# Second block of an output projection by seven products, with other places and queues around it

## The chip, the cores and the metric

The kernel runs on one core of a Trainium2 chip. The metric is the device time of one execution in microseconds (us). The engines are named as in the profile: PE multiplies matrices, DVE, ACT and POOL do elementwise work, SP issues most of the DMAs; ACT and POOL have DMA queues of their own.

## The reference

The kernel computes a gated mix of attention and a layer of 64 experts, for 2048 tokens of width 1024. Cut to what matters:

```python
g = sigmoid((x * gate_w).sum(-1, keepdims=True))
q, k, v = split_heads(x @ wqkv)                    # 32 heads of width 32
a = heads(softmax(q k^T / sqrt(32)) @ v) @ wo      # attention, then its output projection
b = sum over heads of gelu(x . u[e]) * v[e]        # e: the best of 8 x 8 keys of that head
out = g * a + (1 - g) * b
```

## The kernel before, in words

Numbers of 32 bits are split into two parts, hi and lo, by the helper `split` (ACT copies the hi part, L95; DVE subtracts it to get lo, L96). A product of two such numbers is three matmuls: hi by hi, hi by lo, lo by hi.

The program runs through six stages on one core. First the projections of q and k (L291 a first plain piece, L303 the rest), then the router of the experts (L726), the values (L965 and L984), 32 heads of attention (L1319 scores, L1329 exponentials, L1340 weights times values, L1369 row sums), and the output projection (L1522, L1529, L965). The gate and the experts' weighted sum lie among them. PE's order is the order in which the code calls `matmul`; each engine works through its own instructions in that order, and semaphores hold an instruction until what it reads is written and what it overwrites is read. DMAs go by the helper `dma` (L77) on the queue of SP unless another is given, and are issued in the order of the code too; within a queue each issue can wait, and then all behind it wait.

A product of two matrices cut in halves is computed in two ways here. The plain way takes eight products of halves. `Halves` takes seven (P1 to P7): sums of quarters of the left factor (S1 to S4) with sums of quarters of the right factor (T1 to T4), then a chain of additions on DVE (`tt`, L971) that puts the four quarters of the result together:

```python
tt(u2, c1, p6); tt(u3, u2, p7); tt(u2, u2, p5); tt(u5, u3, p5)
```

where `c1` is a copy of P1; `c1` plus P2, `u2` plus P3, `u3` plus P4 and `u5` (in the output stage plus the experts' share) are then stored. P1, P2, P3, P4 use A11, A12, S4, A22; P5, P6, P7 use S1, S2, S3.

**The start.** The first weights are two tiles of 128x128, one that becomes `A` and one that becomes `S` (both `wraw`), on ACT's queue; x comes on SP's. PE multiplies an identity (L409) seven times while they load, as its first work, and then begins L291.

**The values' last unit.** `values_unit(u)` runs for u = 0 to 5. Its results go through four places, `c1`, `u2`, `u3` and `u5` of `work` (in the profile `xh`), and are stored to `vd`. In the last unit (`last`), `first_scores` (L1225) issues the first four matmuls of attention between P2 and P4.

**The output.** The 2048 rows are worked in eight blocks of 256. `wo` is held as `woh` and `wol`, split from `wo_raw`. A block's attention result is loaded as `V` (`OC[n]`, by `load_o`), its reciprocal row sums times the gate as `rb` or `accd` (`RB[n]`, by `load_rb`), and multiplied (L1549, L1576, L1591). The reciprocals of the last group of four heads are the last of all: `norm_r(G - 1)` computes them on DVE (L1402, L1403), a DMA stores them to `rd`, and `load_rb(n, KC - 1, KC)` loads them for the last K step of blocks 0 and 1. Blocks 0 and 1 are computed the plain way (`wo_mm`: eight K steps of 12 matmuls, and eight of `av_mm` for the experts' share, 104 in all); blocks 2 to 7 by `unit(n)` with seven products of 12 and the same eight, 92 in all. The places of the results, `post`, lie in the first block's `rb` and are four pieces of 512: `plain_out` fills all four for blocks 0 and 1, `unit` uses three of them and `osb`. The `T1` to `T4` come from memory (`t0h`, `t0l` to `t3h`, `t3l`, each 1 MB in all or in four pieces).

Of the kernel before, what the change touches and what calls it, by code (L numbers as in the profile page):

```python
# [16 lines left out]
S = 2048  # L17
D = 1024
H = 32
KC = D // 128  # L20
# [11 lines left out]
def gated_mha_peer_kernel(ctx, tc, xT, wqkv, wv, wo, wq, k12, ug, v, out):  # L32
# [42 lines left out]
    def dma(dst, src, queue=nc.sync):  # L75
        a, b = (ap.bitcast(F32) if ap.dtype == F32R else ap for ap in (dst, src))
        return queue.dma_start(a, b)  # L77
# [289 lines left out]
    w0 = wr.tile([128, 2, KC, 128], F32, name="wraw")  # L367
    wraw[0] = raw_quarters(w0)

    def load_w0(k0, k1, queue=nc.sync):  # L370
        for w in range(2):
# [19 lines left out]
    for name in ("B11", "B12", "B21", "B22"):  # L391
        X[name] = x_parts(PASS[0][name], None, xp)

    load_w0(0, 1, nc.scalar)
    load_x(0, 0, 2)
    load_w0(1, 2)
    load_x(0, 1)
# [7 lines left out]
    plain_banks(0)  # L405


    for i in range(7):
        nc.tensor.matmul(b0[1, 1][:, :128], ident, ident, start=True, stop=True)  # L409
    dma(gw, ug.rearrange("p (k m) -> p k m", k=KC)[:, :, 64:65], nc.gpsimd)  # L410
    dma(kraw, k12.rearrange("p (a e) -> p a e", a=2), nc.gpsimd)
# [731 lines left out]
    pso = None  # L1143

    def values_unit(u):
        c1, u2, u3, u5 = (work[k] for k in ("c1", "u2", "u3", "u5"))
        last = u == NU - 1
        order = (("P1", "P2", "P3", "P7", "P5", "P6", "P4") if u == 0 else
                 ("P1", "P7", "P5", "P6", "P3", "P2", "P4") if last else
                 ("P1", "P7", "P5", "P6", "P2", "P3", "P4"))  # L1150
        p, done = {}, set()

        def out(j, half, t, queue=nc.sync):
            dma(VD[half][(2 * u + j) * 128:(2 * u + j + 1) * 128, :], t, queue)

        for k, name in enumerate(order):
            if last and name == "P4":

                nonlocal pso
                ps1.close()  # L1160
                pso = Pool("pso", space=PSUM, side="right")
            p[name] = hv.product(name, bank=pv_bank if last and name == "P4" else None)
            if last and name == "P2":
                first_scores()
            if name == "P1":
                nc.scalar.activation(c1, p[name], AF.Copy)
                hv.rows(x_raw[(u + 1) % 2])
                if u + 2 < NU:
                    load_x_raw(u + 2)
            if name == "P6":  # L1170
                tt(u2, c1, p["P6"])
                tt(u3, u2, p["P7"])
                tt(u2, u2, p["P5"])
                tt(u5, u3, p["P5"])
                out(1, 1, u5)
            if "P6" in p:
                if "P2" in p and "C11" not in p:
                    p["C11"] = tt(c1, c1, p["P2"])
                    out(0, 0, c1)
                if "P3" in p and "C12" not in p:  # L1180
                    p["C12"] = tt(u2, u2, p["P3"])
                    out(0, 1, u2)
            if name == "P4":
                tt(u3, u3, p["P4"])

                out(1, 0, u3, nc.gpsimd if last else nc.sync)

            if u + 1 < NU:
                if k == (4 if u == 0 else 0):
                    hv.parts("A11")  # L1190
                    for s in ("S3", "S1", "S2", "S4"):
                        hv.sums(s)
                    done = {"P1"}
                if k >= 5 or u > 0:
                    for q in ("P7", "P5", "P6", "P2", "P3", "P4"):
# [201 lines left out]
        R[g] = wk.tile([128, 128], F32, name="rr", bufs=1)[:, :64]  # L1397
        dma(R[g], SMD[g].rearrange("j (b m) -> (j b) m", m=64))

    def norm_r(g):  # L1400
        r = R.pop(g)
        nc.vector.reciprocal(r, r)  # L1402
        nc.vector.tensor_mul(r, r, G64)  # L1403
        dma(RD[:, :, g, :].rearrange("j n (q m) -> (j n) q m", m=64), r)


    OC, RB = {}, {}
# [13 lines left out]
    def load_chunk(n, k0, k1, queue=nc.sync):  # L1421
        load_o(n, k0, k1, queue)
        load_rb(n, k0, k1, queue=queue)
# [148 lines left out]
    def scale_o(n):  # L1572

        for k in range(2):
            o = OC[n][:, k * HC:(k + 1) * HC]
            nc.vector.tensor_mul(o, o, RB[n][:, k * HC:(k + 1) * HC])  # L1576
        ht.rows(OC[n])
# [16 lines left out]
    def banks4():  # L1594
        return {(i, half): bank() for i in range(W // 128) for half in range(2)}
# [29 lines left out]
    load_t(2, None, [fin.tile([128, S], F32R, name="t3l")])  # L1625
    OH[1] = zp.tile([128, KC, W], F32R, name="z1")
    OL[1] = wk.tile([128, KC, W], F32R, name="acc")
    split_o(1, 0, HC)
    split_o(0, KC - 1, KC)
    load_o(2, 0, KC)  # L1630
    load_t(0, *([keep.tile([128, S], F32R, name=f"wo_raw{j}")] for j in range(2)))
# [6 lines left out]
    load_t(2, [zp.tile([128, S], F32R, name="z0")], None)  # L1638
    load_t(1, *([keep.tile([128, S], F32R, name=f"wo_raw{2 + j}")] for j in range(2)))
    load_rb(3, 0, KC)  # L1640
    load_o(3, 0, KC)
# [5 lines left out]
    load_t(3, *([part[k][:, 512:] for k in range(HC)] for part in (woh, wol)))  # L1647
    ht.places(wk.tile([128, S], F32R, name="acc"), "A11", "A12")
    ht.places(fin.tile([128, S], F32R, name="s31"), "S3", "S1")
    scale_o(2)  # L1650
    for name in ("A11", "S3", "S1", "A12"):
        ht.operand(name)
    wo_mm(pa1, 1, [KC - 1], False, True)
    ht.places(zp.tile([128, S], F32R, name="z1"), "S2")
    ht.places(wk.tile([128, S], F32R, name="acc"), "S4", "A22")
    load_at(3)
    ht.b.update({f"B{i + 1}{j + 1}": [[part[i * HC + k][:, j * 512:(j + 1) * 512] for k in range(HC)]
                                    for part in (woh, wol)] for i in range(2) for j in range(2)})

    def osb():  # L1660
        return wk.tile([128, 512], F32, name="osb")

    def unit(n):


        u2, u3, u5 = (post[:, i] for i in range(3))
# [7 lines left out]
                    scale_o(n + 1)  # L1674
                ht.operand(name)

        p1 = ht.product("P1")
        c1 = osb()
        nc.scalar.activation(c1, p1, AF.Copy)
        if n == 2:  # L1680
            ht.operand("S2")
            plain_out(1, pa1)
            for name in ("S4", "A22"):
                ht.operand(name)
        if n + 2 < S // W:
            load_chunk(n + 2, 0, KC)
            load_at(n + 2)
        ahead("A11")
        p7 = ht.product("P7")
        ahead("S3")  # L1690
        p5 = ht.product("P5")
        ahead("S1")
# [3 lines left out]
        tt(u2, u2, p5)  # L1696
        tt(u5, u3, p5)
        ahead("S2")

        def c11():  # L1700
            p2 = ht.product("P2", lambda ps: av_mm(n, 0, 0, ps, first=True))
            pieces = 2 if last else 1
            for i in range(pieces):
                c = slice(i * 512 // pieces, (i + 1) * 512 // pieces)
                tt(c1[:, c], c1[:, c], p2[:, c])
                store(n, 0, 0, c1, c)

        def c12():
            p3 = ht.product("P3", lambda ps: av_mm(n, 0, 1, ps, first=True))
# [12 lines left out]
            store(n, 1, 0, u3)  # L1722

        if not last:
            c11()
            ahead("A12")
        c12()
        ahead("S4")
# [43 lines left out]
```

## Time and profile before

| | |
|---|---|
| median of three runs (lowest, highest) | 1823.78 us (1823.51, 1824.25) |
| profiled execution: time | 1824.35 us |
| profiled execution: span | 1822.6 us |
| PE busy in the span | 1813.3 us, 99% |
| DVE, ACT, POOL busy | 1461.6, 1313.3, 228.7 us |

A row of the timeline gives start, duration, engine, line, operation, the names of output and inputs (buffer numbers left out) with their shapes, how many instructions it joins, and in brackets the idle time before it with what ended it. The rows of waits give the engine and line that waited, what for, total us, times, and the longest. Rows of windows give, for a stretch of time, its length, each engine's busy time with its instructions, the granted clock of PE, the share of DMA and the GB/s. SPq, ACTq and POOLq are the parts of an engine that issue DMAs.

### The profile page before, as it was taken

How to read it: one execution, taken by the hardware profiler on the slowest of the kernel's cores; microseconds unless marked ns; L12 is line 12 of the kernel's file. 1: busy time of each engine (PE TensorE's matmuls, PEld its weight loads, DVE VectorE, ACT ScalarE, POOL GpSimd, SP SyncE). 2: the span in 40 equal slices, each digit the busy share in tenths (PEclk: the TensorE clock that was granted, in tenths of full speed). 3: DMA queues.
4: the chain of work that ended last, by engine and by line, in shares of the span. 5: the costliest groups of instructions: out<-in, count | busy, mean ns of one | idle time of the engine just before them, and what ended most of it. 6: DMA issues, size and time to landing. Idle time of an engine off the chain costs nothing.

```text
span 1822.6 us, 26388 instructions
## 1 busy us (share of the span) xinstructions
PE 1813.3 (99%) x10075; PEld 1098.9 (60%) x10075; DVE 1461.6 (80%) x1258; ACT 1313.3 (72%) x1716; POOL 228.7 (13%) x351
## 2 busy tenths in 40 slices
PE   9999999999999999999999999999999999999999
PEld 6777777788888644444444444444444444447887
DVE  7865966789967788888888888888888888897674
ACT  6544644522333699999999999999999999994221
POOL 1222212244101100000000000000000000000000
PEclk9999999999999999999999999999999999999999
DMA  7888689660267778777788877878787778866641
GB/s 267 281 277 277 214 288 295 197 220 13 81 231 245 224 162 181 151 174 167 166 176 173 181 164 175 170 171 189 159 184 171 161 166 181 186 149 239 256 156 58
DMA packets 117072, 345.23 MB, mean 189 GB/s; under 512 B 16112, under 2 KB 49552, under 8 KB 96016
## 3 DMA queue, kind: packets, MB, share of 16 engines
q1 hardware_dynamic: 87608, 196.28, 36.3%
q0 software_dynamic: 27888, 145.00, 34.7%
q10 hardware_dynamic: 1448, 2.24, 0.3%
q8 instruction: 80, 1.31, 0.3%
q14 instruction: 48, 0.39, 0.1%
HBM read 171.76 MB, written 72.36 MB: 134 GB/s over the span
## 4 chain that ended last, share of the span: by engine, by line
PE 94%; issue 2%; DVE 2%; DMA 1%; ACT 0%; POOL 0%; ACTq 0%; DVEq 0%; POOLq 0%; SPq 0%
PE ring L1319 29%; PE o L1340 26%; PE bk L303 15%; PE pa L965 6%; PE bk L726 5%; PE bk L291 3%; PE pa L1522 2%; PE bk L984 2%; PE bk L965 2%; PE bk L342 2%; PE ring L1353 1%; PE pa L1529 1%; DVE xh L971 1%; DMA t1l<-xl 1%; PE bk L191 0%
## 5 line engine op out<-in xcount | busy, mean ns | idle before, releaser
L1329 ACT ACTIVATE P<-ring 128x1024 f32<-128x1024 f32 (+2 forms) x1031 | 913.1, 983 | 13.1
L1369 DVE TENSOR_TENSOR acc<-acc,P 128x2048 f32<-128x2048 f32 x319 | 731.0, 2292 | 74.5 <-ACT P L1329 49.0
L1340 PE MATMUL o<-P,V 128*32 128x512 f32 x3840 | 464.8, 599 | 0.0
L1319 PE MATMUL ring<-Q,K 98*128 98x512 f32 x1024 | 271.7, 407 | 0.1
L1319 PE MATMUL ring<-z,z 98*128 98x512 f32 x1020 | 270.4, 407 | 0.6 <-ACT accd L1329 0.6
L1319 PEld LDWEIGHTS ring<-Q,K 98*128 98x128 f32 x1024 | 182.1, 188 | 143.7 <-ACT P L1329 73.5
L1319 PEld LDWEIGHTS ring<-z,z 98*128 98x128 f32 x1020 | 181.5, 188 | 142.3 <-ACT P L1329 72.3
L1340 PEld LDWEIGHTS o<-P,V 128*32 128x32 f32 x3840 | 98.8, 109 | 223.4 <-issue 214.5
L1362 POOL DMA_DIRECT2D accd<-P x95 | 81.5, 858 | 928.4 <-PE ring L1319 303.8
L1367 DVE TENSOR_TENSOR acc<-P,P 128x2048 f32<-128x2048 f32 x32 | 73.4, 2293 | 72.5 <-ACT P L1329 72.5
L303 PE MATMUL bk<-xh,A 128*128 128x512 f32 x336 | 82.8, 396 | 0.0
L303 PE MATMUL bk<-xh,S 128*128 128x512 f32 x336 | 81.3, 393 | 0.0
L303 PE MATMUL bk<-xl,S 128*128 128x512 f32 x336 | 80.1, 391 | 0.0
L136 ACT ACTIVATE hi<-u 128x512 fp32r<-128x512 f32 x42 | 26.5, 632 | 72.8 <-DVE u L513 36.1
L303 PEld LDWEIGHTS bk<-xh,A 128*128 128x128 f32 x336 | 62.0, 188 | 23.8 <-issue 5.0
L1372 DVE TENSOR_TENSOR acc<-acc,accd 128x2048 f32<-128x2048 f32 x32 | 73.1, 2285 | 0.0
L303 PEld LDWEIGHTS bk<-xl,S 128*128 128x128 f32 x336 | 62.8, 188 | 16.3 <-issue 1.7
L303 PEld LDWEIGHTS bk<-xh,S 128*128 128x128 f32 x336 | 62.4, 188 | 14.5 <-issue 1.7
L1329 ACT ACTIVATE accd<-ring 128x1024 f32<-128x1024 f32 (+2 forms) x64 | 62.2, 1032 | 2.3 <-PE ring L1319 2.2
L965 PE MATMUL pa<-woh,acc 128*128 128x512 f32 x192 | 62.2, 389 | 0.0
L513 DVE TENSOR_TENSOR u<-u,bk 128x512 f32<-128x512 f32 x70 | 46.6, 683 | 12.2 <-DMA wpd<-u 7.6
L730 ACT ACTIVATE xu<-bk 128x64 f32<-128x64 f32 x16 | 3.6, 223 | 61.4 <-PE bk L726 61.4
(301 smaller groups left out, 2209.6 us busy)
## 6 DMA issues: line engine op xcount, KB each, us to landing
accd<-P POOLq DMA_DIRECT2D x95, 1024.0 KB, 7.8
wqt<-in_wq SPq DMA_DIRECT2D x64, 512.0 KB
wraw<-in_wqkv SPq DMA_DIRECT2D x28, 512.0 KB
kdh<-hi POOLq DMA_DIRECT2D x32, 256.0 KB, 6.3
kdl<-lo POOLq DMA_DIRECT2D x32, 256.0 KB, 7.0
qdh<-hi POOLq DMA_DIRECT2D x32, 256.0 KB, 6.6
qdl<-lo POOLq DMA_DIRECT2D x32, 256.0 KB, 6.5
z<-kdh SPq DMA_DIRECT2D x32, 256.0 KB
```

What stands on the lines that cost most here:

```text
L291: nc.tensor.matmul(b0[w, n], AW[PLAIN[w, ki]][a][:, k, :], X[f"B{ki + 1}{n + 1}"][b][:, k, :], start=first, stop=last)
L303: nc.tensor.matmul(ps, a[i][:, k, :], b[j][:, k, :], start=(k == 0 and i == j == 0), stop=(k == HC - 1 and i == 1))
L513: nc.vector.tensor_tensor(out=out, in0=a, in1=b, op=OP.add)
L726: nc.tensor.matmul(ps, x_part(a, t // 4, kc)[:, tok], b, start=first, stop=last)
L965: nc.tensor.matmul(ps, self.a[a][i][:, k, :], self.b[b][j][k], start=(not first and k == 0 and i == j == 0), stop=(k == HC - 1 and i == 1))
L1319: on_ring(nc.tensor.matmul(ring[:, i, :], K[:98, kt * 128:(kt + 1) * 128], Q[:98, qc * 512:(qc + 1) * 512], start=True, stop=True), i)
L1329: on_ring(nc.scalar.activation(P[h, kt][:, q0 * 512:(q0 + m) * 512].rearrange("p (a m) -> p a m", a=m), ring[:, i:i + m, :], AF.Exp, scale ...
L1340: nc.tensor.matmul(O[h][32 * qc:32 * qc + 32, :], Vt[g][:, kt, 32 * j:32 * j + 32], p[:, qc * 512:(qc + 1) * 512], start=(kt == 0), stop=( ...
L1362: nc.gpsimd.dma_start(ACCD[h], P[h, kt], accum_op=OP.add)
L1367: nc.vector.tensor_add(ACC[h], P[h, 0], P[h, kt])
L1369: nc.vector.tensor_add(ACC[h], ACC[h], P[h, kt])
L1372: nc.vector.tensor_add(ACC[h], ACC[h], ACCD[h])
```

## The change

It has three parts.

1. At the start, the tile that becomes `S` goes on SP's queue, ahead of x, and the one that becomes `A` stays on ACT's; the identity is multiplied eight times.
2. In the values' last unit the four places lie in a buffer of raw x that is free by then (`xw`), not in `work`.
3. In the output, block 1 goes by `unit(1)`. Its P1 and P7 stand ahead of block 0's last K step. Its sum of P1 and P2 goes to the fourth piece of `post` and is made right after P1 and P2, ahead of the next block's scaling. The last reciprocals are stored and loaded on POOL's queue. The other loads stand on SP's queue in another order: all of block 1 at once, T3, T1, T2, then T4 ahead of block 0's stores.

The core of the diff:

```diff
-    load_w0(0, 1, nc.scalar)
+    load_w0(0, 1, (nc.scalar, nc.sync))
...
-    for i in range(7):
+    for i in range(8):
         nc.tensor.matmul(b0[1, 1][:, :128], ident, ident, start=True, stop=True)
...
     def values_unit(u):
+        last = u == NU - 1
         c1, u2, u3, u5 = (work[k] for k in ("c1", "u2", "u3", "u5"))
+        if last:
+            free = x_raw[(u + 1) % 2].rearrange("p k m -> p (k m)").rearrange("p (a m) -> p a m", m=512)
+            c1, u2, u3, u5 = (free[:, k] for k in range(4))
...
-    def norm_r(g):
+    def norm_r(g, queue=nc.sync):
...
-        dma(RD[:, :, g, :].rearrange("j n (q m) -> (j n) q m", m=64), r)
+        dma(RD[:, :, g, :].rearrange("j n (q m) -> (j n) q m", m=64), r, queue)
...
-            load_o(1, 0, KC - 1)
+            load_o(1, 0, KC)
+            load_o(0, KC - 1, KC)
+            load_t(2, [zp.tile([128, S], F32R, name="z1")], [fin.tile([128, S], F32R, name="t3l")])
...
         if kc == HC:
-            norm_r(G - 1)
+            norm_r(G - 1, nc.gpsimd)
+            load_t(0, *([keep.tile([128, S], F32R, name=f"wo_raw{j}")] for j in range(2)))
     for n in range(2):
-        load_chunk(n, KC - 1, KC)
-    load_rb(2, 0, KC)
+        load_rb(n, KC - 1, KC, nc.gpsimd)
     split_lo(KC - 1)
     split(woh[0], wol[0], raw_wo(0))
...
+    load_t(1, *([keep.tile([128, S], F32R, name=f"wo_raw{2 + j}")] for j in range(2)))
...
+    scale_o(1, 0)
+    for name in ("A11", "S3"):
+        ht.operand(name)
+    load_rb(2, 0, KC)
...
     for (i, half), ps in pa.items():
         av_mm(0, i, half, ps)
+    early = ht.product("P1"), ht.product("P7")
     wo_mm(pa, 0, [KC - 1], False, True)
-    split_o(1, HC, KC)
+    scale_o(1, 1)
+    for name in ("A12", "S1"):
+        ht.operand(name)
     load_at(2)
...
-    pa1 = banks4()
-    wo_mm(pa1, 1, list(range(KC - 1)), True, False)
-    for (i, half), ps in pa1.items():
-        av_mm(1, i, half, ps)
-    plain_out(0, pa)
     load_t(3, *([part[k][:, 512:] for k in range(HC)] for part in (woh, wol)))
+    plain_out(0, pa)
...
-    wo_mm(pa1, 1, [KC - 1], False, True)
...
+        def c11():
+            p2 = ht.product("P2", lambda ps: av_mm(n, 0, 0, ps, first=True))
...
+            r = post[:, 3] if n == 1 else c1
...
+        if n == 1:
+            c11()
         ahead("A11")
-        p7 = ht.product("P7")
+        p7 = p7 or ht.product("P7")
...
-    for n in range(2, S // W):
-        unit(n)
+    for n in range(1, S // W):
+        unit(n, *(early if n == 1 else ()))
```

In the values' last unit DVE's rows stand as follows, before. The `bk` and `o` are PE's products, and the six rows from L971 are the seven additions of the last unit.

```order
L96 TENSOR_TENSOR xl0_4607<-xl0_4607,xu_4609 128x512 x2
L971 TENSOR_TENSOR xh3_4587<-xh3_4587,bk1_5393 128x512
L971 TENSOR_TENSOR xh3_4587<-xh3_4587,bk7_5367 128x512
L971 TENSOR_TENSOR xh3_4587<-xh3_4587,bk0_5380 128x512 x2
L971 TENSOR_TENSOR xh3_4587<-xh3_4587,bk2_5411 128x512
L971 TENSOR_TENSOR xh3_4587<-xh3_4587,bk3_5426 128x512
L971 TENSOR_TENSOR xh3_4587<-xh3_4587,o_5462 128x512
```

And the same place now:

```order
L96 TENSOR_TENSOR xl0_4608<-xl0_4608,xu_4610 128x512 x2
L971 TENSOR_TENSOR xw_4450<-xw_4450,bk1_5394 128x512
L971 TENSOR_TENSOR xw_4450<-xw_4450,bk7_5368 128x512
L971 TENSOR_TENSOR xw_4450<-xw_4450,bk0_5381 128x512 x2
L971 TENSOR_TENSOR xw_4450<-xw_4450,bk2_5412 128x512
L971 TENSOR_TENSOR xw_4450<-xw_4450,bk3_5427 128x512
L971 TENSOR_TENSOR xw_4450<-xw_4450,o_5463 128x512
```

Nothing has moved; the places are others.

In the output stage SP's queue stood as follows from the last reciprocals on (`rr` is read back for them, `rd` is where they are stored, `V` a block's attention result).

```order
L77 DMA V<-od 128x1792
L77 DMA rd<-rr 32x4x64
L77 DMA V<-od 128x256
L77 DMA rb_5491<-rd 128x1x256
L77 DMA V<-od 128x256
L77 DMA accd<-rd 128x1x256
L77 DMA accd<-rd 128x1x2048
L77 DMA t3l<-t2l 128x2048
L77 DMA V<-od 128x2048
L77 DMA wo_raw_12582<-t0h 128x2048
L77 DMA wo_raw_12583<-t0l 128x2048
```

Now it stands so, up to the stores of block 0 (behind `V<-od 128x2048` of block 2 follow an `at`, the eight pieces of T4 and then `out<-rb_5492 128x512 x4`):

```order
L77 DMA V<-od 128x2048
L77 DMA V<-od 128x256
L77 DMA z_12462<-t2h 128x2048
L77 DMA t3l<-t2l 128x2048
L77 DMA wo_raw_12535<-t0h 128x2048
L77 DMA wo_raw_12536<-t0l 128x2048
L77 DMA wo_raw_12576<-t1h 128x2048
L77 DMA wo_raw_12577<-t1l 128x2048
L77 DMA accd<-rd 128x1x2048
L77 DMA V<-od 128x2048
```

The three transfers of the reciprocals left SP's queue; POOL's last rows, behind its DMAs of attention, are now:

```order
L1365 DMA accd<-P_12216 128x2048
L1365 DMA accd<-P_12241 128x2048
L77 DMA rd<-rr 32x4x64
L77 DMA rb_5492<-rd 128x1x256
L77 DMA accd<-rd 128x1x256
```

So SP no longer waits for them, and POOL does.

On PE the rows from the experts' share of block 0 (`at` times `vhl`) on were, before, followed at once by block 0's last K step:

```order
L1529 MATMUL pa0_12411<-vhl_5490,at_12454 128x512 x2
L1529 MATMUL pa1_12412<-vhl_5490,at_12454 128x512 x2
L1529 MATMUL pa2_12413<-vhl_5490,at_12454 128x512 x2
L1529 MATMUL pa3_12414<-vhl_5490,at_12454 128x512 x2
L1522 MATMUL pa0_12411<-woh7_12401,z0_12263 128x512
L1522 MATMUL pa1_12412<-woh7_12401,z0_12263 128x512
```

Now P1 of block 1 comes there, then P7, and only then that K step:

```order
L1532 MATMUL pa0_12412<-vhl_5491,at_12455 128x512 x2
L1532 MATMUL pa1_12413<-vhl_5491,at_12455 128x512 x2
L1532 MATMUL pa2_12414<-vhl_5491,at_12455 128x512 x2
L1532 MATMUL pa3_12415<-vhl_5491,at_12455 128x512 x2
L965 MATMUL pa4_12607<-woh0_12410,acc_12580 128x512
L965 MATMUL pa4_12607<-wol0_12411,acc_12580 128x512
```

24 matmuls have moved ahead of the last K step of block 0.

More of the change, by code (lines that the diff above doesn't have):

```diff
@@ L368, in gated_mha_peer_kernel, with load_w0 @@
     wraw[0] = raw_quarters(w0)
-    def load_w0(k0, k1, queue=nc.sync):
-        for w in range(2):
+    def load_w0(k0, k1, queues=(nc.sync, nc.sync)):
+        for w, queue in enumerate(queues):
             dma(w0[:, w, k0:k1], wqkv[w * 8, :, k0 * 128:k1 * 128].rearrange("p (k m) -> p k m", m=128),
@@ L1570, in load_t, with scale_o @@
             ops[n] = [place[:, k * 512:(k + 1) * 512] for place in part for k in range(m)]
-    def scale_o(n):
-        for k in range(2):
+    def scale_o(n, *ks):
+        for k in ks or range(2):
             o = OC[n][:, k * HC:(k + 1) * HC]
@@ L1615, in gated_mha_peer_kernel @@
         if kc == HC:
-            norm_r(G - 1)
+            norm_r(G - 1, nc.gpsimd)
+            load_t(0, *([keep.tile([128, S], F32R, name=f"wo_raw{j}")] for j in range(2)))
     for n in range(2):
-        load_chunk(n, KC - 1, KC)
-    load_rb(2, 0, KC)
+        load_rb(n, KC - 1, KC, nc.gpsimd)
     split_lo(KC - 1)
     split(woh[0], wol[0], raw_wo(0))
[L1625 to L1628, printed above, removed]
+    load_t(1, *([keep.tile([128, S], F32R, name=f"wo_raw{2 + j}")] for j in range(2)))
+    ht.b.update({f"B{i + 1}{j + 1}": [[part[i * HC + k][:, j * 512:(j + 1) * 512] for k in range(HC)]
+                                    for part in (woh, wol)] for i in range(2) for j in range(2)})
+    ht.places(wk.tile([128, S], F32R, name="acc"), "A11", "A12")
+    ht.places(fin.tile([128, S], F32R, name="s31"), "S3", "S1")
+    scale_o(1, 0)
+    for name in ("A11", "S3"):
+        ht.operand(name)
+    load_rb(2, 0, KC)
     split_o(0, KC - 1, KC)
     load_o(2, 0, KC)
-    load_t(0, *([keep.tile([128, S], F32R, name=f"wo_raw{j}")] for j in range(2)))
     ps_odd = Pool("ps_odd", space=PSUM)
@@ L1634, in gated_mha_peer_kernel, with unit @@
         av_mm(0, i, half, ps)
+    early = ht.product("P1"), ht.product("P7")
     wo_mm(pa, 0, [KC - 1], False, True)
-    split_o(1, HC, KC)
+    scale_o(1, 1)
+    for name in ("A12", "S1"):
+        ht.operand(name)
     load_at(2)
[L1638 to L1641, printed above, removed]
-    pa1 = banks4()
-    wo_mm(pa1, 1, list(range(KC - 1)), True, False)
-    for (i, half), ps in pa1.items():
-        av_mm(1, i, half, ps)
-    plain_out(0, pa)
[L1647 to L1652, printed above, removed]
-    wo_mm(pa1, 1, [KC - 1], False, True)
-    ht.places(zp.tile([128, S], F32R, name="z1"), "S2")
+    load_t(3, *([part[k][:, 512:] for k in range(HC)] for part in (woh, wol)))
+    plain_out(0, pa)
+    ht.places(zp.tile([128, S], F32R, name="z0"), "S2")
     ht.places(wk.tile([128, S], F32R, name="acc"), "S4", "A22")
-    load_at(3)
-    ht.b.update({f"B{i + 1}{j + 1}": [[part[i * HC + k][:, j * 512:(j + 1) * 512] for k in range(HC)]
-                                    for part in (woh, wol)] for i in range(2) for j in range(2)})
     def osb():
         return wk.tile([128, 512], F32, name="osb")
-    def unit(n):
+    def unit(n, p1=None, p7=None):
         u2, u3, u5 = (post[:, i] for i in range(3))
@@ L1675, in ahead @@
                 ht.operand(name)
-        p1 = ht.product("P1")
+        def c11():
+            p2 = ht.product("P2", lambda ps: av_mm(n, 0, 0, ps, first=True))
+            pieces = 2 if last else 1
+            r = post[:, 3] if n == 1 else c1
+            for i in range(pieces):
+                c = slice(i * 512 // pieces, (i + 1) * 512 // pieces)
+                tt(r[:, c], c1[:, c], p2[:, c])
+                store(n, 0, 0, r, c)
+        p1 = p1 or ht.product("P1")
         c1 = osb()
         nc.scalar.activation(c1, p1, AF.Copy)
[L1680 to L1683, printed above, removed]
+        if n == 1:
+            for name in ("S2", "S4", "A22"):
                 ht.operand(name)
@@ L1687, in unit @@
             load_at(n + 2)
+        if n == 1:
+            c11()
         ahead("A11")
-        p7 = ht.product("P7")
+        p7 = p7 or ht.product("P7")
         ahead("S3")
@@ L1698, in unit @@
         ahead("S2")
[L1700 to L1706, printed above, removed]
         def c12():
@@ L1724, in unit @@
         if not last:
-            c11()
+            if n > 1:
+                c11()
             ahead("A12")
```

1 line of the change is left out of this document (removed).

## Prediction

> **What bounds the kernel now.** I read the page first: the busy line and the chain of work that ended last.
>
> ```profile
> PE 1813.3 (99%) x10075; PEld 1098.9 (60%) x10075; DVE 1461.6 (80%) x1258; ACT 1313.3 (72%) x1716; POOL 228.7 (13%) x351
> PE 94%; issue 2%; DVE 2%; DMA 1%; ACT 0%; POOL 0%; ACTq 0%; DVEq 0%; POOLq 0%; SPq 0%
> ```
>
> PE is busy in all but 9.3 of 1822.6 us. The next view is PE's waits, in five stretches; 19 to 200, 640 to 1640 and 1640 to the end have no row. 0 to 20 and 200 to 640 have these:
>
> ```profile
> PE bk L291 <- ACT xh L95: 2.1, 1, 2.1
> ...
> PE bk L1225 <- DVE xh L971: 1.0, 1, 1.0
> PE ring L1319 <- ACT accd L1329: 0.6, 1, 0.6
> ```
>
> So from its first real matmul on PE is the bound everywhere, the output included. A microsecond of PE's work or waiting that goes is a microsecond of the end, and a new wait counts in full. I price each part by what it does to PE.
>
> **The start.** The timeline of the first microseconds:
>
> ```profile
> 0.76 0.87 SPq L77 DMA_DIRECT2D xh<-in_xT  x2
> 0.77 0.90 ACTq L77 DMA_DIRECT2D wraw<-in_wqkv  x2
> 1.40 3.36 PE L409 MATMUL bk<-ident 128*128 128x128 f32 x14 [1.40 <-DVE ident L91]
> 4.89 0.31 ACT L95 ACTIVATE A<-wraw 128x128 fp32r<-128x128 f32 x1 [1.91 <-DMA wraw<-in_wqkv]
> 5.25 0.43 SPq L77 DMA_DIRECT2D xh<-in_xT  x1
> 5.96 0.31 ACT L95 ACTIVATE S<-wraw 128x128 fp32r<-128x128 f32 x1 [0.77 <-DMA wraw<-in_wqkv]
> 6.18 1.14 ACT L95 ACTIVATE xh<-xh 128x512 fp32r<-128x512 f32 x2
> 6.84 0.73 PE L291 MATMUL bk<-xh,A 128*128 128x512 f32 x2 [2.08 <-ACT xh L95]
> ```
>
> PE waits for x's hi part; ACT makes that third, after `A` and `S`, and `S` waits for its tile. First on a queue of its own the tile should land with `A`'s, so that `S` follows at about 5.2. x then goes out one issue later (0.43); its first half had landed by 5.25, where SP goes on after a wait that I put to it, so now by 5.7. From ACT's start on x to PE is 6.84 - 6.18 = 0.66. The first matmul comes between 5.42 + 0.66 = 6.1 and 5.7 + 0.66 = 6.36, or at 6.84 if the tile comes no sooner. I take 6.1, a gain of 0.74.
>
> The idle time matters for something else, in the windows:
>
> ```profile
> 7.00:8.00 1.00, 1.00 (x5) 0.82 (x6) 1.00 (x2) 0.95 (x4) 0.72 (x2) 1.00 1.05 362
> 8.00:9.00 1.00, 1.00 (x5) 0.82 (x4) 1.00 (x4) 1.00 (x3) 0.63 (x3) 0.67 1.04 348
> 9.00:10.00 1.00, 1.00 (x3) 0.73 (x3) 1.00 (x3) 0.68 (x3) 0.00 (x0) 0.50 0.99 295
> 10.00:11.00 1.00, 1.00 (x4) 0.78 (x3) 0.93 (x3) 1.00 (x3) 0.00 (x0) 0.50 1.03 336
> 11.00:12.00 1.00, 1.00 (x5) 0.76 (x4) 1.00 (x3) 1.00 (x3) 0.00 (x0) 0.63 1.02 397
> 612.00:615.00 3.00, 1.99 (x9) 1.28 (x9) 2.96 (x5) 1.61 (x4) 0.00 (x0) 1.00 0.40 162
> ```
>
> The granted clock is half for some 3.4 us (0.33 + 0.50 + 0.50 + 0.37 = 1.70 us of full speed lost) after the idle 2.08 us; after 1.01 us idle near 613 it stayed at 1.00. The eighth identity (3.36 / 7 = 0.48) ends at 5.24, so that 0.86 us of idle is left, less than what cost nothing at 613. So I take the slow stretch to go: 1.70. A faster PE meets x's later pieces: ACT starts on the fourth at 12.80, released by its DMA; I leave 0.25 for such waits. The start gives 0.74 + 1.45 = 2.2, and 0.7 if the clock still falls.
>
> [...]
>
> **The values' last unit.**
>
> ```profile
> 609.57 0.68 DVE L971 TENSOR_TENSOR xh<-xh,bk 128x512 f32<-128x512 f32 x1
> 611.87 3.20 DVE L971 TENSOR_TENSOR xh<-xh,bk 128x512 f32<-128x512 f32 x5 [1.62 <-DMA vd<-xh]
> 612.29 0.63 PE L1225 MATMUL bk<-z,z 98*128 98x512 f32 x2
> 613.93 0.73 PE L1225 MATMUL bk<-z,z 98*128 98x512 f32 x2 [1.01 <-DVE xh L971]
> ```
>
> PE's third score matmul needs a bank that DVE's additions free, and these wait for the stores of the unit before, which still read the same places. In other places DVE goes on at 610.25; the additions take 0.64 each (3.20 / 5), and the one that frees the bank, the fourth in all, ends at about 612.2. The third matmul would follow the second: 612.29 + 2 x 0.227 = 612.74, not 613.93. Gain 1.2 (bounds 0.9 and 1.2); the new place is free, since no unit follows. The next row of PE's waits (0.6 at L1319, for ACT) may take up to 0.3 of it.
>
> **The output.** The cost of a matmul is in the chain of waits; then what block 1 and the reciprocals rest on:
>
> ```profile
> 1711.88 13.60 PE pa L965 x60
> ...
> 1656.18 0.60 SPq L77 DMA_DIRECT2D rd<-rr  x1
> 1659.37 0.54 SPq L77 DMA_DIRECT2D rb<-rd  x1
> 1661.61 1.22 DVE L1591 TENSOR_TENSOR V<-V,accd 128x1024 f32<-128x1024 f32 x1
> 1665.48 1.98 PE L1529 MATMUL pa<-vhl,at 128*128 128x512 f32 x8
> 1667.29 1.07 PE L1522 MATMUL pa<-woh,z 128*128 128x512 f32 x4
> ```
>
> 13.60 / 60 = 0.2267. Block 1 takes 92 instead of 104: 12 x 0.2267 = 2.72.
>
> *Covers.* In before's time P1 would run from 1667.29, P7 from 1670.0, block 0's last K step from 1672.7 to 1675.45. P1's factor is ready at about 1664.2 (1661.61 and 1.22 for the scaling, then two parts of a 128x512 tile, 0.68 each as the addition of that size below). The reciprocals on POOL: they were sent at 1656.18; POOL's queue is empty by then. Its transfers take, from issue to landing,
>
> ```profile
> t0h<-xh POOLq DMA_DIRECT2D x4, 256.0 KB, 2.6
> accd<-P POOLq DMA_DIRECT2D x95, 1024.0 KB, 7.8
> ```
>
> I take 5 for each of the two in turn, about the middle, since they are small but SP's queue is full: landed at about 1667, and 1671.7 would do (K step at 1672.7 less about 1.0 for DVE's and ACT's parts). At 7.8 each it is 1671.8, just in time: cost nothing to 0.1.
>
> *The new wait.* The sum of P1 and P2 of block 1 goes to the fourth piece of `post`, from which block 0's fourth store reads. DVE can't begin it until that store has landed, and behind it on DVE stand block 2's scaling, its operands, and the additions that free PE's bank for block 2's P7. The stores now stand behind T4 in SP's queue. How fast that empties:
>
> ```profile
> SPq L77 <- DMA accd<-rd: 3.4, 1, 3.4
> SPq L77 <- DMA V<-od: 2.4, 1, 2.4
> SPq L77 <- DMA wo_raw<-t1h: 2.1, 1, 2.1
> SPq L77 <- DMA wo_raw<-t1l: 2.0, 1, 2.0
> ...
> 1652.97 0.38 SPq L77 DMA_DIRECT2D V<-od  x1
> ```
>
> Each with the issue of about 0.35 that follows: 1 MB takes 2.4, `V` 2.75, `accd` 3.8. `V` of block 1, issued at 1652.97, lands at about 1658 by the 5 us above; six of 1 MB to 1672.6, `accd` to 1676.4, `V` to 1679.2, `at` 0.35, T4 (2 MB) to 1684.4, the stores to about 1686.8; without gaps in the first part some 1685. DVE could otherwise go on at about 1681.7, after P2.
>
> What follows on DVE in a block:
>
> ```profile
> 1702.05 2.35 DVE L1576 TENSOR_TENSOR V<-V,accd 128x1024 f32<-128x1024 f32 x2
> 1709.08 0.68 DVE L971 TENSOR_TENSOR rb<-osb,pa 128x512 f32<-128x512 f32 x1
> 1709.79 2.01 DVE L971 TENSOR_TENSOR rb<-rb,pa 128x512 f32<-128x512 f32 x3
> ```
>
> From scaling to the second addition's end is 8.4 (1702.05 to 1710.46); with the sum itself (0.68) 9.1. A landing at 1684.5 would free P7's bank at 1693.6, where block 2's P7 is due (1667.29 + 116 x 0.2267: three times 12 to the K step's end, the other 68 of block 1 and 12 of block 2's P1). From 1684.5 on each later microsecond is a stall; 1684.5 to 1687.5 gives 0 to 3, and I take 1.5. The output gives 2.7 - 1.5 = 1.2 (bounds +2.7 and -0.5). T4, which P4 of block 1 needs at about 1687.7, has landed by 1684.4; nothing else of block 1 is later.
>
> **Sum.** 2.2 + 1.2 + 1.2 = 4.6. The profiled execution took 1824.35 (1822.6 and 1.75 outside the span) and so would take 1819.75; it lies 0.57 above the median, so the median becomes 1823.78 - 4.6 = 1819.2.
>
> **The rivals.**
>
> *The clock falls all the same* (chance 0.15). Against it: less idle time than the 1.01 at 613, which cost nothing. For it: that is one case, in another phase. Gain 0.7 + 1.2 + 1.2 = 3.1: 1820.7.
>
> *The stores come so late that the twelve matmuls are eaten* (chance 0.13). SP's queue moves over 9 MB ahead of them; every gap in it adds. With a landing from 1687.2 to 1689.1 the output gives 0 to -1.9, and the time is 1820.4 to 1822.3.
>
> *Slower: the reciprocals on POOL come too late* (chance 0.06). PE stands at block 0's last K step with nothing in front but P1 and P7, and DVE's queue stands too, at the scaling by `rb`. PE waits from a landing at 1671.7 on. To eat 2.2 + 1.2 + 2.7 = 6.1 it must come at 1677.8, and to be slower by more than 0.2% (3.65 us) at 1681.5: 12.7 per transfer, against 2.6 to 7.8 in the rows. At 13.5 each the time is 1829. SP's full queue beside it speaks for it, the rows, taken beside much traffic too, against.
>
> *The change does not do what it says at 613* (chance 0.02), since the additions wait for something else than the places: 1.2 less, 1820.4. The row's releaser, a store to `vd`, speaks against.
>
> **How the numbers follow.** A measurement can tell about 0.2%, so faster means below 1820.1. The forecast has 0.64: 1817.7 without stall, 1820.7 with all of 3; 0.59 of it is faster, and 0.05 comes from the first rival, where the clock falls but no stall comes (1819.2). The rest of that rival, the second and the last lie between 1820.4 and 1822.3, so the same. That makes 0.64 faster, 0.30 the same, 0.06 slower. The range goes from 1817.2 (every term at its better bound, 2.5 + 1.2 + 2.7, would be 1817.4) to 1822.0, which leaves out the slower case and the end of the second rival.
>
> **What would show it.** Right: the first L291 at about 6.1 with a clock of 1.00 through the first 15 us; the second pair of L1225 without a wait; a row of PE waiting at L965 of 0 to 3 us at about 1690, released by DVE; no wait at the last K step of block 0. Wrong: a clock of 0.50 again, a wait at `S`, a PE wait at L1525, or one of more than 3 us in the output.

## The result, and the profile after

The change makes the kernel slower: 1827.08 us in the median of 17 runs (1825.30 to 1829.89), against 1823.88 of before in as many; the ratio is 1.0018, interval 1.0011 to 1.0025. The profiled execution of after took 1826.49 us with a span of 1824.4; that of before had 1824.35 and 1822.6. It is one of the quicker executions of after, so the two traces differ by 2.1 us where the medians differ by 3.2.

The busy line and PE's waits of the changed kernel, those of the first 20 us, then those from 1640 us to the end (line, who is waited for, total us, times, longest):

```profile
PE 1812.6 (99%) x10065; PEld 1097.1 (60%) x10065; DVE 1470.1 (81%) x1273; ACT 1314.8 (72%) x1720; POOL 229.8 (13%) x354
...
PE bk L291 <- ACT xh L95: 1.6, 2, 1.2
...
PE pa L965 <- ACT acc L95: 2.1, 1, 2.1
PE pa L965 <- DVE rb L971: 1.3, 1, 1.3
PE pa L965 <- DVE acc L96: 0.3, 1, 0.3
```

PE has ten records fewer (twelve matmuls less, and two records for the eighth identity), and less busy time. The wait at L1225 is gone. But the output, where PE never waited before, now has three waits. They lie together, at the passage from block 1 to block 2. The timeline of the changed kernel there (start, duration, engine, line, output and inputs, in brackets the idle time before and what ended it):

```profile
1688.71 0.69 DVE L971 TENSOR_TENSOR rb<-osb,pa 128x512 f32<-128x512 f32 x1 [8.48 <-PE pa L965]
1689.32 2.35 DVE L1579 TENSOR_TENSOR V<-V,accd 128x1024 f32<-128x1024 f32 x2
1690.57 0.63 ACT L95 ACTIVATE acc<-V 128x512 fp32r<-128x512 f32 x1 [11.15 <-DVE V L1579]
1691.25 0.50 PE L965 MATMUL pa<-woh,acc 128*128 128x512 f32 x1 [2.12 <-ACT acc L95]
1692.33 1.22 PE L965 MATMUL pa<-woh,acc 128*128 128x512 f32 x2 [0.34 <-DVE acc L96]
1696.96 2.01 DVE L971 TENSOR_TENSOR rb<-rb,pa 128x512 f32<-128x512 f32 x3
1697.80 0.47 PE L965 MATMUL pa<-z,s 128*128 128x512 f32 x1 [1.34 <-DVE rb L971]
```

This reads as follows. The first row is the sum of P1 and P2 of block 1, which writes the fourth piece of `post` (`rb`). DVE stood idle for 8.48 us before it. The row puts that down to PE, whose P2 had ended some twelve us earlier (P5, which comes next, began at 1676.73): it is one of those waits in which the engine named had long been done. What DVE did wait for, the experiments show. Block 2's scaling (L1579) and its A11 (ACT, L95) follow at once, and PE's P1 of block 2 at 1691.25, then, after the chain of additions, its P7 at 1697.80.

How much was lost is read from places that both traces have: the start of the experts' share of block 0 and PE's last matmul. In the changed kernel:

```profile
1663.58 1.98 PE L1532 MATMUL pa<-vhl,at 128*128 128x512 f32 x8
...
1820.07 0.39 PE L965 MATMUL pa<-woh,acc 128*128 128x512 f32 x1
```

and the last matmul before:

```profile
1818.48 0.39 PE L965 MATMUL pa<-woh,acc 128*128 128x512 f32 x1
```

PE began the experts' share of block 0 at 1663.58 instead of 1665.48, so the first two parts had won 1.90 (0.61 by 609 us, 1.20 at L1225). Twelve matmuls fewer are 2.72 more. By these P7 of block 2 was due at 1693.6 - 1.90 = 1691.7, with 1693.6 the prediction's time for it. It came at 1697.80: 6.1 us lost, against 4.6 won. The difference, 1.5, is what the last matmul shows: it starts 1.59 later.

### The profile page after: what moved, and what is told of

It reads as the page before. It is cut to its first block, busy times and chain, and to the rows that moved or that the text cites. A ratio compares the mean times of both kernels' runs of the same rounds, so it can differ in the third digit from the quotient of the medians.

```text
span 1824.4 us, 26392 instructions
## 1 busy us (share of the span) xinstructions
PE 1812.6 (99%) x10065; PEld 1097.1 (60%) x10065; DVE 1470.1 (81%) x1273; ACT 1314.8 (72%) x1720; POOL 229.8 (13%) x354
## 4 chain that ended last, share of the span: by engine, by line
PE 98%; DVE 0%; ACT 0%; DMA 0%; issue 0%; SPq 0%; DVEq 0%; ACTq 0%
PE ring L1322 29%; PE o L1343 26%; PE bk L303 15%; PE pa L965 7%; PE bk L965 6%; PE bk L726 5%; PE bk L984 2%; PE bk L291 2%; PE bk L342 2%; PE ring L1356 1%; PE pa L1525 1%; PE pa L1532 1%; PE bk L191 0%; DMA xh<-in_xT 0%; PE bk L359 0%; ACT P L1332 0%
## 5 line engine op out<-in xcount | busy, mean ns | idle before, releaser
L965 PE MATMUL pa<-woh,acc 128*128 128x512 f32 x224 | 74.2, 396 | 2.5 <-ACT acc L95 2.1
L95 ACT ACTIVATE acc<-V 128x512 fp32r<-128x512 f32 x28 | 17.1, 626 | 47.7 <-DVE V L1579 19.6
```

The lines of the kernel that those rows point to most:

```text
L965: nc.tensor.matmul(ps, self.a[a][i][:, k, :], self.b[b][j][k], start=(not first and k == 0 and i == j == 0), stop=(k == HC - 1 and i == 1))
```

## The experiments

**The place of the sum.** Is it the write into the fourth piece of `post` that holds DVE? The sum was left in the tile of P1's copy. (The later sums of block 1 read that copy, so three quarters of block 1 hold another sum here; the run is read for its time.)

```diff
-            r = post[:, 3] if n == 1 else c1
+            r = c1
```

> The changed kernel, with the sum of P1 and P2 of block 1 left in the tile that holds P1's copy instead of the fourth piece of post. Theory (DVE's queue stands at that sum until block 0's fourth store has landed; block 2's scaling and first operand are behind it): PE's waits at block 2's P1 and P7 and the slow clock at 1690 to 1700 go, 6 us less than the changed kernel, about 1819.4 us, 4.5 below before. Rival (block 2's operands come late because the loads stand in another order, whatever DVE does): at least 2 us of waiting stay at P1, 1825 us or more.

Measured: 1820.47 us, ratio 0.9984 (0.9975 to 0.9993), and no row of PE waiting in the output. The theory holds and the rival falls. The same with a second tile of the `osb` kind, so that all four quarters hold their own sums:

```diff
-            r = post[:, 3] if n == 1 else c1
+            r = osb() if n == 1 else c1
```

> The changed kernel, with the sum of P1 and P2 of block 1 in a second tile of the osb kind instead of the fourth piece of post: the same output as the reference. Theory (only the place held DVE): as with the sum in place, 1820.5 us, no PE wait in the output. Rival (the second tile makes P1's copy of block 2 wait, and PE with it): a PE wait at block 2 and 1822 us or more.

Measured: 1820.10 us, ratio 0.9982 (0.9973 to 0.9991), again no such wait. In its timeline DVE no longer stops at the sum:

```profile
1679.86 0.68 DVE L971 TENSOR_TENSOR osb<-osb,pa 128x512 f32<-128x512 f32 x1
1680.46 2.35 DVE L1579 TENSOR_TENSOR V<-V,accd 128x1024 f32<-128x1024 f32 x2
```

The sum runs 8.85 us earlier than in the changed kernel. Against before, one place makes the difference between 3.2 us lost and 3.65 won.

**Each part alone.** Before with one part of the change at a time (the three parts of the diff above).

> Before with the change at the start alone. Theory (x's second K step, not the weights or the clock, sets PE's pace there): 0.6 us below before, about 1823.3 us, with no clock of 0.5 but an idle PE of about 1.2 us at 9 us. Rival (the prediction's sum): 2.2 us below, 1821.7.

> Before with the last values unit's places alone. Theory (the wait of 1.0 us at L1225 is for the stores from those places): 1.2 us below before, about 1822.7 us, and no row of PE waiting for DVE there. Rival (PE then waits for something next in line): the same as before.

> Before with the change in the output alone. Theory (all of the loss is in the output: 12 matmuls won, 2.7 us, and some 6.2 lost to the wait for the store and the slow clock behind it): 3.5 us above before, about 1827.4 us, and a PE wait of 2 us at block 2's P1. Rival (the wait comes about only because PE got there earlier by the other two parts): 0 to 1.5 above before.

Measured, against 1824.11 of before: the start alone 1822.84 (0.9995, 0.9986 to 1.0004), the places alone 1822.77 (0.9991, 0.9982 to 1.0000), the output alone 1828.34 (1.0025, 1.0016 to 1.0035). The whole loss is in the output, without the other two parts as well. The first two come out as gains of about 1.3 each in the medians; their intervals reach to no change, so neither is shown by its time alone. The start's median lies between its theory and its rival and settles neither. For the places the trace shows it: the wait of 1.0 at L1225 is gone. But that wait is not the same in every execution with the old places: it is 1.0 in before and with the output alone, 1.4 with the eleven identities below, and 0.2 with the start alone. So what the places are worth varies, and part of the start's 1.3 may come from there: in its trace PE begins L191, the end of the first four K steps, at 19.66, against 19.59 in before.

**How the stall grows with the landing.** The prediction had a formula for it: P7 of block 2 starts 9.1 us after the fourth store of block 0 has landed. Three kernels with the sum still in the fourth piece of `post` test it. In one the stores go ahead of all of T4, in one ahead of half of it, and in one DVE scales block 2 and makes its A11 ahead of the sum.

```diff
# stores ahead of T4
-    load_t(3, *([part[k][:, 512:] for k in range(HC)] for part in (woh, wol)))
     plain_out(0, pa)
+    load_t(3, *([part[k][:, 512:] for k in range(HC)] for part in (woh, wol)))
# half of T4 ahead
-    load_t(3, *([part[k][:, 512:] for k in range(HC)] for part in (woh, wol)))
+    load_t(3, [woh[k][:, 512:] for k in range(HC)], None)
     plain_out(0, pa)
+    load_t(3, None, [wol[k][:, 512:] for k in range(HC)])
# A11 ahead of the sum
+        ahead("A11")
         if n == 1:
             c11()
-        ahead("A11")
```

> The changed kernel, with block 0's four stores ahead of T4's eight pieces on SP's queue, the sum still in the fourth piece of post. Theory (the place of the stores in the queue sets when DVE goes on): the fourth store lands some 4 us earlier, the waits at block 2's P1 and P7 go, 1820 to 1821 us; T4 lands 2.4 us later, so that P4 of block 1 may wait up to 2 us, 1822.5. Rival (the stores are late by PE's and ACT's evictions, not by what stands ahead of them): as the changed kernel, 1827.

> The changed kernel, with only T4's four hi pieces ahead of block 0's stores and the four lo pieces behind them (1 MB less ahead). Theory (block 2's P7 starts 9.1 us after the fourth store lands: 0.7 for the sum and 8.4 from scaling to the addition that frees the bank): the store lands some 2.5 us earlier than in the changed kernel, and 2.5 of the 6.1 us lost come back: about 1824.6 us. Rival (a wait that is there or not, or P4 that now waits for T4's lo pieces and loses the same): 1827 us, or 1820.5.

> The changed kernel, with block 2's scaling and first operand A11 ahead of the sum of P1 and P2 on DVE, the sum still in the fourth piece of post. Theory: PE's wait at block 2's P1 goes, that at its P7 comes 0.7 + 5.5 = 6.2 us after the landing instead of 9.1, so that 3 us come back: 1824.1 us; if PE's idle of then some 3 us makes the clock fall and that is paid in full, 1825.8. Rival (the wait at P1 is what costs, with the clock behind it): 1820.5 to 1821.5.

The timelines, first with the stores ahead of T4, then with half of T4 ahead, then with A11 ahead of the sum. In each the first row is the sum and the last the first matmul of block 2's P7:

```profile
1684.34 0.69 DVE L971 TENSOR_TENSOR rb<-osb,pa 128x512 f32<-128x512 f32 x1 [3.55 <-DMA out<-rb]
1693.43 0.47 PE L965 MATMUL pa<-z,s 128*128 128x512 f32 x1
```

```profile
1685.15 0.69 DVE L971 TENSOR_TENSOR rb<-osb,pa 128x512 f32<-128x512 f32 x1 [4.90 <-DMA out<-rb]
...
1694.25 0.47 PE L965 MATMUL pa<-z,s 128*128 128x512 f32 x1 [1.82 <-DVE rb L971]
```

```profile
1688.04 0.69 DVE L971 TENSOR_TENSOR rb<-osb,pa 128x512 f32<-128x512 f32 x1 [5.27 <-DMA out<-rb]
...
1694.25 0.47 PE L965 MATMUL pa<-z,s 128*128 128x512 f32 x1 [2.97 <-DVE rb L971]
```

Here the releaser is named as what it is, the store (`DMA out<-rb`). Against before, measured alongside, the ratios are 0.9987 (0.9978 to 0.9996) for the stores ahead of T4, 1.0007 (0.9998 to 1.0016) for half of T4 ahead and 1.0006 (0.9997 to 1.0015) for A11 ahead of the sum. From the sum to P7:

| kernel | sum starts | P7 expected | P7 seen | median us |
|---|---|---|---|---|
| changed kernel | 1688.71 | +9.1 = 1697.81 | 1697.80 | 1827.08 |
| output alone | 1690.63 | +9.1 = 1699.73 | 1699.71 | 1828.34 |
| half of T4 ahead | 1685.15 | +9.1 = 1694.25 | 1694.25 | 1825.06 |
| stores ahead of T4 | 1684.34 | +9.1 = 1693.44 | 1693.43 | 1821.24 |
| A11 ahead of the sum | 1688.04 | +6.2 = 1694.24 | 1694.25 | 1824.90 |

The formula is right to 0.02 us in all five. It also says what the wait at P1 is worth: with A11 ahead of the sum that wait is gone, and P7 waits 2.97 instead; the time is far from the 1820.5 to 1821.5 that the rival wanted. T4 behind the stores costs little: 0.2 us with half of it there (the row of PE waiting for `wol`), and some 0.7 with all of it there, where twelve matmuls took 3.40 instead of 2.72 (1687.08 to 1690.48). With half of T4 ahead the landing was 3.6 earlier instead of the expected 2.5, and the time 2.0 below the changed kernel's instead of 2.5; the clock, below, takes the rest. The second half of T4 brought only 0.8 more (1685.15 to 1684.34), or 1.5 if the later start of that execution is taken off (L191 at 19.74 instead of 19.08). So the landing does not move in proportion to the bytes ahead of it; why is not shown.

**The clock.** In the changed kernel, with half of T4 ahead and with A11 ahead of the sum, the windows after the wait (length, busy time of PE, PEld, DVE, ACT, POOL, granted clock, DMA share, GB/s) show:

```profile
1692.00:1694.00 2.00, 1.68 (x4) 1.39 (x5) 1.30 (x3) 0.63 (x1) 0.00 (x0) 0.58 0.33 127
1694.00:1696.00 2.00, 2.00 (x6) 1.57 (x6) 1.22 (x3) 0.63 (x1) 0.00 (x0) 0.57 0.01 3
```

```profile
1694.00:1696.00 2.00, 1.75 (x6) 1.46 (x7) 1.97 (x4) 0.00 (x0) 0.00 (x0) 0.77 0.01 3
1696.00:1698.00 2.00, 2.00 (x7) 1.52 (x6) 1.22 (x3) 1.15 (x2) 0.00 (x0) 0.50 0.00 0
1698.00:1700.00 2.00, 2.00 (x9) 1.65 (x8) 1.29 (x3) 0.59 (x2) 0.00 (x0) 0.88 0.22 87
```

```profile
1694.00:1696.00 2.00, 1.75 (x8) 1.47 (x9) 1.97 (x4) 0.00 (x0) 0.00 (x0) 1.00 0.00 0
1696.00:1698.00 2.00, 2.00 (x11) 1.64 (x9) 1.22 (x3) 1.15 (x2) 0.00 (x0) 1.00 0.00 0
```

In the changed kernel the slow clock lies between P1 and P7, where PE would have waited for DVE anyway: P7 came when the formula says, so it was not paid. With half of T4 ahead it comes behind P7 (0.46 + 1.00 + 0.24 = 1.70 of full speed) and is paid nearly in full: with A11 ahead of the sum P7 begins at the same 1694.25, and the last matmul at 1816.55 instead of 1818.12, 1.57 earlier. With A11 ahead the slow clock did not come there in the profiled execution, of 1822.99 us, although PE had stood for 2.97; eleven executions went from 1822.99 to 1827.55.

Only one execution of each kernel has a trace, but every execution has its mean granted clock on record, and one slow stretch is 1.70 of some 1824 us, or 0.0009. With A11 ahead the two slowest (1827.38 and 1827.55) have 0.998 and the others 0.999 or 1.000. Of the 17 executions of the changed kernel the ten up to 1827.14 have 0.999, and of the seven from 1828.04 on six have 0.998 or 0.997. So the slower ones go with more of the slow clock, and the median of the changed kernel stands further above before's than its trace does. Where the clock fell in them is not shown.

**The start.** Eleven identities instead of seven, so that PE has no idle time to speak of, and nothing else:

```diff
-    for i in range(7):
+    for i in range(11):
```

> Before with eleven identities instead of seven at the start, nothing else: they end at 6.7 us, PE is idle for some 0.2 us ahead of the first real matmul, which comes at 6.8 to 7.0 as before. Theory (x's landing sets PE's pace in the first 12 us, and the clock's loss is only hidden in that): no clock of 0.5, but an idle PE of about 1 us ahead of the second K step, and 0.5 us below before at most. Rival (the 1.7 us of the slow clock were lost time): 1.7 us below before.

Measured: 1823.47 against 1823.75 (0.9998, 0.9989 to 1.0007). The median speaks for the theory, but the interval doesn't rule the rival out, and the trace speaks against the theory. The start can be read where PE begins L191, behind the first four K steps. With eleven identities it does so at 18.08, 1.51 earlier than before's 19.59 (0.45 of it is an earlier first matmul, at 6.39 instead of 6.84), with no slow clock after that and no row of waiting ahead of the second K step. In before x's second K step was early enough; ACT's row for it, and PE's first row that uses it:

```profile
7.77 1.15 ACT L95 ACTIVATE xh<-xh 128x512 fp32r<-128x512 f32 x2
...
10.88 1.96 PE L291 MATMUL bk<-xh,A 128*128 128x512 f32 x6
```

From ACT to PE takes 0.66, so PE could have had it at 8.4, and came to it at 10.88 with the slow clock of 8.33 to 11.75 upon it. Up to L191 the slow stretch of before was lost time, then. How much of it reaches the end is open: the last matmul with eleven identities starts at 1817.65, 0.83 before before's, and the wait at L1225 is 1.4 instead of 1.0 there.

The two other kernels with an unchanged start have slow matmuls there too. In their windows the clock reads 1.00, but the column also reads 1.00 where a trace has no record of the clock (in before up to 4.92 us). The number of matmuls tells more; the places alone:

```profile
7.00:8.00 1.00, 1.00 (x3) 0.80 (x3) 1.00 (x3) 0.86 (x4) 0.30 (x2) 1.00 1.10 388
...
11.00:12.00 1.00, 1.00 (x6) 0.83 (x5) 1.00 (x3) 0.88 (x2) 0.00 (x0) 1.00 1.01 354
```

PE was busy for all of both, with half as many matmuls in the first. These two kernels begin L191 at 19.20 and 19.64, eight executions with the changed start at 18.49 to 19.74, 19.07 in the mean. So the changed start is worth some 0.4 there, although its first matmul comes 1.2 us and more ahead of before's 6.84, and none of its matmuls behind 7.1 us is slow (in the changed kernel they start 0.23 apart from 7.09 on). What takes the rest is x's second K step: ACT begins on it at 8.60 to 10.04 in the eight, 9.34 in the mean, and at 7.64 to 8.35 in the four with the old queues. The start alone:

```profile
5.44 1.11 PE L291 MATMUL bk<-xh,A 128*128 128x512 f32 x2 [0.26 <-ACT xh L95]
9.93 1.15 ACT L95 ACTIVATE xh<-xh 128x512 fp32r<-128x512 f32 x2 [3.18 <-DMA xh<-in_xT]
10.61 2.29 PE L291 MATMUL bk<-xh,A 128*128 128x512 f32 x6 [1.77 <-ACT xh L95]
```

The first matmul is 1.4 earlier than before's, and PE then stands 1.77 for x's second K step, on which ACT begins at 9.93 (7.77 in before). Why it lands later than before was not tried. Two kernels, both with the sum in the `osb` tile, bring that x sooner:

```diff
# x ahead of the second weights
-    load_w0(1, 2)
     load_x(0, 1)
+    load_w0(1, 2)
# the second weights on ACT's queue
-    load_w0(1, 2)
+    load_w0(1, 2, (nc.scalar, nc.scalar))
```

> The kernel with the sum in a second osb tile, and at the start x's second K step ahead of the second K step's weights on SP's queue. Theory (PE waits for that piece of x): it lands 0.5 to 1 us earlier, PE's second wait gets shorter by as much, 1819.3 us. Rival (the weights, or the DMA engines' pace whatever the order, are as late): 1820.1 as with the order of the change.

> The kernel with the sum in a second osb tile, and at the start the second K step's weights on ACT's queue, so that x's second K step stands right behind the first on SP's. Theory: as with x ahead of the weights, 0.5 to 1 us less, 1819.3 us. Rival (ACT's queue takes its share of the same engines): 1820.1.

Measured: 1819.47 (0.9975, 0.9966 to 0.9984) and 1819.17 (0.9976, 0.9966 to 0.9986), with L191 at 17.97 and 17.44, and ACT at x's second K step at 8.26 and 7.72. Both beat before (1824.08, measured alongside) by 4.6 and 4.9 us; with each other they are even. That they lie 0.6 to 0.9 below 1820.10 is what was expected, but their intervals overlap with that kernel's, so the times alone don't show it. At L191 it can be seen: they are 1.6 and 2.15 earlier there than before, so that most of the 2.2 that the prediction gave to the start is there once x comes in time.

**The reciprocals.** In the kernel with the `osb` tile, the three transfers back on SP's queue:

```diff
-            norm_r(G - 1, nc.gpsimd)
+            norm_r(G - 1)
...
-        load_rb(n, KC - 1, KC, nc.gpsimd)
+        load_rb(n, KC - 1, KC)
```

> The kernel with the sum in a second osb tile, and the three transfers of the last reciprocals on SP's queue, where the code now calls them. Theory (POOL's queue spares them the transfers of T3 and T1): they land 1 to 5 us later than at 1667, PE waits 0 to 3 us at block 0's last K step, 1820.5 to 1824 us. Rival (they are not late on either queue): the same as with POOL's queue, 1820.5.

Measured: 1821.12 (0.9986, 0.9977 to 0.9995). DVE has the reciprocals at 1669.76, and PE doesn't wait for them; on POOL's queue, in the changed kernel, it had them at 1667.49. So POOL's queue brings them 2.3 earlier, and that is covered on either queue. The spans of the two traces differ by 0.6 (1818.4 against 1817.7), and that is the start (L191 at 19.17 against 18.49). The medians differ by 1.0, because the executions fall into two groups: five of 1820.07 to 1820.43 with a mean clock of 1.000, and six of 1821.12 to 1822.42 with 0.999. Where the clock fell in those six is not shown.

## Why the prediction was wrong

The forecast was 1819.2 and the result is 1827.08. The step that failed is the new wait of the output: the mechanism, the place and the formula were right, and its one input, when block 0's fourth store lands, was mis-sized, so that the term taken as 1.5 measured 6.1. A second term was too large as well: the start, 2.2, of which 0.5 came.

- **The landing.** I had 1685 to 1687.5 in before's time, 1686.8 by the chain, which is 1684.9 in after's, 1.90 ahead. DVE went on at 1688.71, 3.8 later, and each microsecond was a stall as the prediction says: 6.1 instead of 0 to 3 with 1.5 taken. My second rival had the right mechanism and stopped at 4.6.
- **Why it was late.** I chained single transfers from the landing of `V`: 2.4 us each. The windows of the changed kernel (columns as above) show what the DMA engines moved:

```profile
1654.00:1666.00 12.00, 12.00 (x54) 9.93 (x54) 8.90 (x12) 3.58 (x5) 1.70 (x3) 1.00 1.01 417
1666.00:1668.00 2.00, 2.00 (x11) 1.65 (x10) 0.42 (x1) 0.05 (x1) 0.00 (x0) 1.00 1.00 164
1668.00:1678.00 10.00, 10.00 (x46) 8.29 (x45) 6.49 (x10) 3.72 (x7) 0.00 (x0) 1.00 1.00 414
1678.00:1690.00 12.00, 11.13 (x50) 8.88 (x48) 2.82 (x5) 1.15 (x2) 0.00 (x0) 1.00 1.05 398
```

 The share of the DMA engines is full to the stores' landing. SP's timeline there shows the landings, since its next issue waits for them (2.1 us each in its rows of waits), of T2's last tile, of `accd` and of `V`:

```profile
1675.11 0.32 SPq L77 DMA_DIRECT2D wol<-t3l  x1
1677.54 0.32 SPq L77 DMA_DIRECT2D wol<-t3l  x1
1679.97 0.80 SPq L77 DMA_DIRECT2D wol<-t3l  x2
```

 T2's last tile landed at 1675.11, not at 1672.6 - 1.9 = 1670.7. Of the 4.4 between, the two microseconds at 164 GB/s explain 1.2 (2 x (1 - 164/417)). Some 1.7 came back at once: `accd` and `V` then took 4.9 together instead of 6.55, as if part of `accd` had already been moved beside the tiles, which is not shown. The other 1.5 is not accounted for. T4 and the stores took 8.7 instead of 7.6, at 398 GB/s. That makes 4.4 - 1.7 + 1.1 = 3.8.
- **The first waiter.** I looked at P7's bank alone. P1 stood too, for A11, 2.12 us. It changed nothing, since P7 was due to wait longer.
- **The start, 2.2.** The first matmul came sooner than I had it (5.60; 5.44 with the start alone), and the clock stayed up (1.00 in the windows from 7 to 20 us). But I left 0.25 for x's later pieces, taking them to land as before. x's second K step came to ACT at 9.36 instead of 7.77, and PE stood 1.20 for it: L191 began 0.52 earlier (19.07 against 19.59), 0.4 in the mean of the traces. The slow stretch's 1.70 was rightly counted as lost time of before, up to L191 at least; the wait for x took its place.
- **The places, 1.2.** Right: 1.20 (609.49 against 608.88 before the wait, 613.93 against 612.12 = 611.67 + 2 x 0.227 after it). That the wait was the 1.0 of the profile read beforehand is in part luck: with the same places it was 0.2 and 1.4 in two other traces.
- **The twelve matmuls, 2.72.** Right, as the kernel with the `osb` tile shows: its last matmul starts at 1813.40, 5.08 before before's; 2.36 of that it had won by the experts' share of block 0 (1663.12 against 1665.48), and 2.72 is left.
- **The reciprocals on POOL.** Covered, as forecast, though they came later: the two transfers took some 6.5 each instead of 5, from 1654.55 to 1667.49, where 1665.1 was forecast in after's time.
- **The slower rival** was the wrong one. The case on the other side was the store, which I had priced only to the point where it ate the gain.

On the clock: in the traces it fell after 2.08 us of idle PE (before), 2.12 (the changed kernel and the output alone) and 1.82 (half of T4 ahead), and did not after 1.72 (the output alone, ahead of P7), 1.77 (the start alone) and 2.97 (A11 ahead of the sum).

## What to carry to other kernels

Before a result is put into a place that is free "by then", ask who reads it last. If that is a store, ask what stands ahead of it on its queue (here the sum started 3.56 us earlier with half of T4 behind the stores, and 4.37 with all of it), and what stands behind the waiting instruction on its own engine (here DVE stood for 8.48 us, and block 2's scaling started at 1689.32 instead of 1680.46 in the kernel with the `osb` tile). Price such a landing by the bytes and the GB/s of a full window (398 to 417 here), with room for a dip (164 here), not by a chain of single transfers, and price the loss to the end, not to the point where it cancels the gain. At the start, follow the next input that PE needs under the new order of the queues (PE stood 1.20 us for it in the changed kernel) before counting an earlier first matmul as won.

## What was not expected of the hardware

In the traces of before and of the changed kernel the half clock lasted 3.41 us, 1.70 us of full speed (8.33 to 11.75, and 1692.32 to 1695.73). The length of the idle time before it does not tell whether it comes: it came after 1.82 us in one execution and not after 2.97 in another. What decides it is not shown.

Between P1 and P7 of the changed kernel, where PE would have waited anyway, the fall cost nothing (P7 at 1697.80, with 1697.81 by the formula). Behind P7, with half of T4 ahead, it was paid (1.57 at the last matmul), and so it was at the start of before up to L191 (1.51 against the eleven identities, 0.45 of it by their earlier first matmul). And the last two loads of the reciprocals (`rb<-rd` and `accd<-rd` on POOL's queue, issued at 1661.05 and 1661.59, landed after 6.4 and 8.2 us) fell together with the one dip of a full queue, 164 GB/s from 1666 to 1668 with the DMA engines fully busy; what made the dip was not tried.
